# Weight and activation stores moved from SyncE's queue to GpSimd's, with a new instruction order

## The chip, the cores and the metric

The kernel runs on one core of a Trainium2 chip. The metric is the device time of one execution in microseconds (us); lower is better. The core has five engines with an instruction queue each: TensorE (PE, with its weight loads PEld), VectorE (DVE), ScalarE (ACT), GpSimd (POOL) and SyncE (SP). SyncE does nothing but issue transfers between the chip's memory (DRAM) and the on-chip buffers (SBUF); ScalarE and GpSimd can issue transfers too. Each queue runs strictly in its order: an instruction that waits holds back all behind it on its queue.

## The reference

Two layers, each with a windowed attention and a feed-forward part, on 2048 tokens of 1024 values, in bfloat16:

```python
x = x + A(layernorm(x)); x = x + B(layernorm(x))      # twice, with the same weights

def A(x):      # 32 heads of 32, window of 8 keys, 2 tokens apart
    q, k, v = split(x @ wqkv)
    logits[s, w] = (q[s] . k[s - 2 * w]) / sqrt(32)   # masked where s - 2 * w < 0
    o = sum over w of softmax(logits)[s, w] * v[s - 2 * w]
    return o @ wo

def B(x):
    return relu(x @ w1 + b1) ** 2 @ w2 + b2           # w1 is 1024 x 3584
```

## The kernel before

The tokens are split by parity, so that a window becomes eight neighbours, and worked on in blocks of 512: four blocks a layer, eight units `u` in all. A unit runs through layer norm and transposes (`SA`), the projections to q, k and v (`SQ`, `SQ7`), the attention on VectorE with logits and row sums on TensorE (`S2`), the output projection (`SW`, `SW7`), and the two feed-forward products (`SF1`, `SF2`). The attention of unit u + 1 is interleaved with the feed-forward part of unit u, so that VectorE and TensorE are both busy.

Most products use a form of Strassen's scheme with seven instead of eight sub-products. Its combined weights are made once, in units 0 and 1: VectorE forms four combinations of each weight tile in buffers named `tv` (`keep_wqkv`, `keep_w1`, `keep_w2`, `keep_wo`; at most four `tv` buffers live at a time), a store writes each to a scratch tensor in DRAM, and later units load them back from there into weight buffers `w`. The scratch tensors show in the profile as `sk` and `sqv` (q, k, v), `sw` (w1), `tw` (w2) and `two` (wo). The other stores are those of the layer's output: `xs` between the layers and `out_dram` at the end, both written from `xm` by `out_tile`, 128 tokens at a time; the last four token tiles are stored in halves of a row. There are 88 stores of scratch and 37 of layer outputs, some of these of half a row or less; the very last piece is issued from ScalarE, all others from SyncE.

In unit 0 the attention sums its products of q and k over the eight channel tiles with a tree of additions on VectorE before the logits' matmuls (`lg`) on TensorE. `DEP0` gives the depth of that tree for the first and the second half of the block: depth 2 leaves two sums, and so two times four matmuls, depth 3 one sum and four matmuls. All other units use depth 3 in both halves. The row sums of unit 0's softmax are matmuls as well (`den`).

No instruction is placed by hand. Every step is recorded in a `Plan` with its engine, a cost and what it reads and writes. `schedule` then plays the plan: at each moment a free engine takes the ready step of the lowest priority number for which buffers are free. A transfer may start only where at most `LANES` = 7 others have not landed by the plan's own reckoning, and it takes its bandwidth from one shared stream. `emit` first shifts priorities at random, by the seeds of `ORDER`, and replays; the seeds have been searched for a short plan. The order in which steps are taken is the order of each engine's queue in the program. So a changed cost or limit moves instructions on every engine. `dma` records a transfer; its argument `eng` names the issuing queue.

Of the kernel before, what the change touches and what calls it, by code (L numbers as in the profile page):

```python
# [45 lines left out]
KEEP = {"k": 0, "q": 1, "v": 1}  # L46
WO7 = (2, 3, 4, 5, 6)
KWO = 1
DEP0 = (2, 3)
NEARLY = 4  # L50
PLAIN1 = 1
HALF = 8
# [7 lines left out]
FNO = True  # L60
CPA = (1,)
AFTK = True
TAIL = True
CPT = ("xn3",)
PR1 = 20.0
# [3 lines left out]
GZ = 6  # L69

ORDER = [
# [9 lines left out]

MM = 0.2157
MMH = 0.1091
# [4 lines left out]
LANES = 7  # L88
# [45 lines left out]
class Plan:  # L134
# [45 lines left out]
    def schedule(self):  # L180
# [17 lines left out]
            fresh.add(item[2].eng)  # L198

        def fits(o):  # L200
            if o.mb and len(landed) >= LANES and landed[-LANES] > t + 1e-9:
                return False
            need = {}
            for b in o.bufs:
                if b.slot is None:
                    need[b.cls] = need.get(b.cls, 0) + 1
                    if b.tag in self.caps and (live.get(b.tag, 0) >= self.caps[b.tag] or b.idx != placed.get(b.tag, 0)):
                        return False
                    if b.bits == "seeded" and partial.issuperset(free["ps"]):
                        return False  # L210
            return all(len(free[c]) >= n for c, n in need.items())
# [15 lines left out]
            if o.ndep == 0:  # L227
                offer((o.prio, next(seq), o))
        dma_free = 0.0
        landed = []  # L230
        out = []
        t = 0.0
        left = len(self.ops)
        while left:
            progress = False
            for e in engs:
                if efree[e] > t + 1e-9 or e not in fresh:
                    continue
                i = next((i for i, item in enumerate(ready[e]) if fits(item[2])), None)
                if i is None:  # L240
                    fresh.discard(e)
                    continue
                o = ready[e].pop(i)[2]
                progress = True
                for b in o.bufs:
                    if b.slot is None:
                        take(b)
                efree[e] = t + o.dur
                end = t + o.dur
                if o.mb:  # L250
                    dma_free = max(dma_free, end) + o.mb / DMA_MBS
                    end = dma_free
                    landed.append(end + o.lat)
                out.append((t, len(out), o))
                left -= 1
                heapq.heappush(events, (efree[e], next(seq), None, False))
                if not o.mb:
                    heapq.heappush(events, (end + OWN_LAT.get(o.eng, 0.0), next(seq), o, True))
                heapq.heappush(events, (end + o.lat, next(seq), o, False))
# [5 lines left out]
            t, _, o, own = heapq.heappop(events)  # L265
# [72 lines left out]
class _Kernel:  # L338
# [84 lines left out]
    def dma(self, out, src, r, w, mb, prio=None, after=(), name="dma", cast=None, lat=None, eng="SP", dur=None):  # L423
        def fn():
            o = out()
            (self.nc.sync if eng == "SP" else self.nc.scalar).dma_start(o if cast is None else o.bitcast(cast), src())
        return self.p.add(eng, dur or 0.08, fn, r, w, self.nxt() if prio is None else prio, after, mb=mb, name=name, lat=lat)

    def par_tile(self, par_ap, t):
        cls = t // (self.NT // 2)  # L430
# [22 lines left out]
    def keep_w2(self, j0, n, w):  # L453
        nc, p = self.nc, self.p
        t = [Buf("2K", "tv", [128, 2, BLK], F16) for _ in range(4)]

        def raw(k2, n2):
            return w[:, k2, n2, :n]

        def comb(i, a, b, r):  # L460
            p.add("DVE", dve(n * BLK), lambda: nc.vector.tensor_tensor(t[i][:, :n], a(), b(), ALU.subtract), r, [(t[i], 0)], 45.0, name="tv")
            self.dma(lambda: self.tw[i][:, j0:j0 + n, :], lambda: t[i][:, :n], [(t[i], 0)], [(("tw", i), j0)], n * 0.13, prio=50.0, name="twst", lat=4.0)
        comb(0, lambda: raw(0, 1), lambda: raw(0, 0), [(w, 0)])
        comb(1, lambda: raw(1, 1), lambda: t[0][:, :n], [(w, 1), (t[0], 0)])
        comb(2, lambda: raw(1, 1), lambda: raw(0, 1), [(w, 0), (w, 1)])
        comb(3, lambda: raw(1, 0), lambda: t[1][:, :n], [(w, 1), (t[1], 0)])
# [56 lines left out]
    def keep_wqkv(self, nm, ws, after=()):  # L523
# [4 lines left out]
        def one(s):  # L528
# [5 lines left out]
            def comb(t, a, b, op, r, pr):  # L534
                p.add("DVE", dve(1024), lambda: nc.vector.tensor_tensor(t[:], a(), b(), op), r, [(t, 0)], self.nxt(), after, name="tq")
                i = COMB.index(pr)
                self.dma(lambda: self.scr[job][nm, s][:, i], lambda: t[:], [(t, 0)], [((job, nm, s), i)], 0.26, prio=50.0, name="wqst", lat=4.0)
            w0, w1 = (ws[0], s), (ws[1], s)
            comb(s1, lambda: raw(1, 0), lambda: raw(1, 1), ALU.add, [w1], 5)
            comb(s3, lambda: raw(0, 0), lambda: raw(1, 0), ALU.subtract, [w0, w1], 7)  # L540
# [130 lines left out]
    def keep_w1(self, dp, w):  # L671
# [5 lines left out]

        def store(pr, src, r):
            i = COMB.index(pr)
            self.dma(lambda: self.scr["w1"][dp][:, i], src, r, [(("w1", dp), i)], 0.26, prio=50.0, name="w1st", lat=4.0)  # L680
        s1, s3, s2, s4 = t = [Buf("2K", "tv", [128, 4, 256], F16) for _ in range(4)]

        def comb(t, a, b, op, r, pr):
# [419 lines left out]
    def keep_wo(self, wos):  # L1103
# [5 lines left out]
        for c0 in (0, 2):  # L1109
            t = [Buf("2K", "tv", [128, 2, BLK], F16) for _ in range(4)]  # L1110

            def comb(i, a, b, r, t=t, c0=c0):
                p.add("DVE", dve(1024), lambda: nc.vector.tensor_tensor(t[i][:], a(), b(), ALU.subtract), r, [(t[i], 0)], 45.0, name="tv")
                self.dma(lambda: self.two[i // 2][:, i % 2, c0:c0 + 2, :], lambda: t[i][:], [(t[i], 0)], [(("two", i // 2), (i % 2, c0))], 0.26,
                         prio=50.0, name="twst", lat=4.0)
            w0, w1 = (wos[0], 0), (wos[1], 0)
            comb(0, lambda c0=c0: raw(0, 1, c0), lambda c0=c0: raw(0, 0, c0), [w0])
            comb(1, lambda c0=c0: raw(1, 1, c0), lambda t=t: t[0][:], [w1, (t[0], 0)])
# [336 lines left out]
    def out_tile(self, layer, t, db, py, xm, end=False):  # L1455
# [19 lines left out]
            return  # L1475
        self.merge(py, lambda: xm[:, sl], lambda: o()[:, sl], [(xm, db)], [(xm, db)], "xo")
        if final and t >= self.NT - 4:
            self.dma(lambda: dst[:, sl], lambda: o()[:, sl], [(xm, db)], [(cell, db)], 0.14, prio=-10.0)
        elif t in self.half:
            self.dma(lambda: dst, lambda: o(), [(xm, 0), (xm, 1)], [(cell, 0), (cell, 1)], 0.27, prio=-10.0)  # L1480
            self.half.discard(t)
        else:
            self.half.add(t)
# [135 lines left out]
```

## Time and profile before

| | us |
|---|---|
| timed runs, median of 3 (lowest to highest) | 1136.02 (1134.17 to 1136.22) |
| the profiled execution's own time | 1131.52 |
| its span, first to last instruction | 1129.8 |
| TensorE busy (share of the span) | 1118.8 (99%) |
| VectorE busy | 990.3 (88%) |
| ScalarE busy | 824.1 (73%) |
| GpSimd busy | 1.8 (0%) |
| mean granted TensorE clock | 0.999 |
| moved by DMA, mean | 362.35 MB, 321 GB/s |

A page of the profile lists the busy time of each engine, groups of instructions by line, tiles and shapes (with the mean ns of one, the idle time of the engine before them, and what ended it), and transfers with the median time from issue to landing. Names such as `w<-tw` say what is written from what. `SPq` is SyncE's queue. The tables of waits name the waiting engine and line, the releaser, and then us in total, the number of waits and the longest. The busy time of matmuls overlaps the next one's, as their ends are modelled, so a mean of one is longer than its place in the row; a row of several in a timeline gives the place.

### The profile page before, as it was taken

How to read it: one execution, taken by the hardware profiler on the slowest of the kernel's cores; microseconds unless marked ns; L12 is line 12 of the kernel's file. 1: busy time of each engine (PE TensorE's matmuls, PEld its weight loads, DVE VectorE, ACT ScalarE, POOL GpSimd, SP SyncE). 2: the span in 40 equal slices, each digit the busy share in tenths (PEclk: the TensorE clock that was granted, in tenths of full speed). 3: DMA queues.
4: the chain of work that ended last, by engine and by line, in shares of the span. 5: the costliest groups of instructions: out<-in, count | busy, mean ns of one | idle time of the engine just before them, and what ended most of it. 6: DMA issues, size and time to landing. Idle time of an engine off the chain costs nothing.

```text
span 1129.8 us, 20632 instructions
## 1 busy us (share of the span) xinstructions
PE 1118.8 (99%) x7854; PEld 770.4 (68%) x7900; DVE 990.3 (88%) x1517; ACT 824.1 (73%) x1648; POOL 1.8 (0%) x8
## 2 busy tenths in 40 slices
PE   9999999999999999999999999999999999999998
PEld 6645764678746887468864788557884678845864
DVE  8999989999996999969999699997999899996341
ACT  7747995598975799567994769847798468933961
POOL 0000000000000000000000000000000000000000
PEclk9999999999999999999999999999999999999999
DMA  9956799999999986999789998999969999689981
GB/s 360 313 193 232 247 312 341 313 352 391 346 367 376 360 333 241 360 418 341 294 285 315 403 318 333 301 382 380 378 230 337 374 360 402 205 290 330 352 300 65
DMA packets 137022, 362.35 MB, mean 321 GB/s; under 512 B 67418, under 2 KB 68570, under 8 KB 116570
## 3 DMA queue, kind: packets, MB, share of 16 engines
q1 hardware_dynamic: 136778, 360.95, 91.4%
q8 instruction: 62, 1.02, 0.4%
q14 instruction: 38, 0.31, 0.1%
q10 hardware_dynamic: 144, 0.07, 0.0%
HBM read 314.84 MB, written 31.46 MB: 307 GB/s over the span
## 4 chain that ended last, share of the span: by engine, by line
PE 72%; DVE 15%; ACT 7%; DMA 3%; issue 2%; SPq 0%; DVEq 0%
PE X L667 19%; PE X L1393 12%; PE Z L667 10%; PE pq L893 6%; PE Z L1393 6%; PE Y L667 5%; PE py L1089 4%; DVE P L955 3%; PE Y L1393 3%; PE X L1160 3%; DVE P L963 3%; ACT r L1328 2%; DVE pr L1034 2%; PE Z L1160 1%; ACT rr L1334 1%
## 5 line engine op out<-in xcount | busy, mean ns | idle before, releaser
L667 PEld LDWEIGHTS <-w 128*128 128x128 f16 (+1 forms) x4904 | 479.8, 98 | 69.6 <-issue 0.5
L1393 PEld LDWEIGHTS <-r 128*128 128x128 f16 x1183 | 115.8, 98 | 135.4 <-issue 1.1
L1393 PE MATMUL X<-w,r 128*128 128x512 f16 (+2 forms) x782 | 176.3, 377 | 0.6 <-ACT X L502 0.2
L955 DVE TENSOR_TENSOR P<-q,k 128x2048 f16<-128x2048 f16 x128 | 154.4, 1230 | 2.4 <-ACT q L630 2.4
L667 PE MATMUL X<-T,w 128*128 128x256 f16 x1224 | 151.7, 273 | 0.0
L1034 DVE TENSOR_TENSOR pr<-pb,v 128x4096 f16<-128x4096 f16 x64 | 146.4, 2298 | 0.5 <-PE X L1393 0.2
L963 DVE TENSOR_TENSOR P<-P,P 128x2048 f16<-128x2048 f16 x111 | 136.1, 1228 | 0.2
L1328 ACT ACTIVATE r<-rr 128x1024 f16<-128x1024 f16 x110 | 123.8, 1137 | 0.3
L1041 DVE TENSOR_TENSOR pr<-pr 128x1024 f16<-128x1024 f16 (+1 forms) x128 | 118.0, 956 | 0.1
L667 PE MATMUL X<-TA,w 128*128 128x256 f16 x864 | 108.4, 273 | 0.0
L893 PE MATMUL pq<-xnA,w 128*128 128x256 f16 (+1 forms) x512 | 86.6, 326 | 1.3 <-DMA w<-in_A_wqkv_dram 0.8
L600 ACT COPY Y<-X 128x512 f32<-128x512 f32 x115 | 71.2, 619 | 18.8 <-PE X L667 14.9
L893 PEld LDWEIGHTS <-w 128*128 128x128 bf16 x512 | 49.7, 98 | 33.5 <-issue 1.3
L1307 ACT CAST y<-Z 128x512 f16<-128x512 f32 x110 | 68.8, 642 | 4.8 <-PE Z L667 4.8
L1311 DVE TENSOR_TENSOR rr<-u,y 128x512 f16<-128x512 f16 x110 | 46.3, 428 | 22.9 <-ACT y L1307 14.5
L1334 ACT ACTIVATE rr<-Y,b1T 128x256 f16<-128x256 f32 x110 | 55.4, 537 | 3.8 <-PE Y L667 3.2
L667 PE MATMUL Y<-xnB,w 128*128 128x256 f16 x440 | 56.4, 273 | 0.0
L1062 ACT CAST yxo<-X 128x512 f16<-128x512 f32 x27 | 15.4, 587 | 56.0 <-PE X L1393 56.0
L1334 ACT ACTIVATE rr<-X,b1T 128x256 f16<-128x256 f32 x110 | 55.2, 559 | 0.7 <-PE X L667 0.5
L618 ACT CAST u<-X 128x512 f16<-128x512 f32 x72 | 41.8, 587 | 18.8 <-PE X L667 17.4
L667 PE MATMUL X<-xnB,w 128*128 128x256 f16 x440 | 55.5, 273 | 0.0
L622 ACT CAST yq<-Z 128x512 f16<-128x512 f32 x72 | 41.9, 586 | 18.4 <-PE Z L667 18.0
(168 smaller groups left out, 1692.0 us busy)
## 6 DMA issues: line engine op xcount, KB each, us to landing
w<-sw SPq DMA_DIRECT2D x49, 1024.0 KB, 9.9
w<-tw SPq DMA_DIRECT2D x56, 896.0 KB, 6.8
w<-in_B_w_dram SPq DMA_DIRECT2D x42, 896.0 KB, 5.8
w<-in_B_w_dram SPq DMA_DIRECT2D x35, 1024.0 KB, 9.4
w<-in_A_wqkv_dram SPq DMA_DIRECT2D x32, 1024.0 KB, 9.9
w<-sqv SPq DMA_DIRECT2D x24, 1024.0 KB, 11.2
w<-in_B_w_dram SPq DMA_DIRECT2D x28, 512.0 KB, 6.5
w<-sk SPq DMA_DIRECT2D x12, 1024.0 KB, 7.8
```

Of the source, the lines that this page charges most:

```text
L600: self.p.add("ACT", act(512), lambda: self.nc.scalar.copy(Y[:], X[:]), [(X, 0)], [(Y, 0)], UP, name="u")
L667: nc.tensor.matmul(bank[:, a, :], lw[:, k, a * 128:(a + 1) * 128], rhs(k), start=(start and k == 0 and a == 0), stop=(k == 3), skip_group_ ...
L893: nc.tensor.matmul(pq[:, t0 * HB:t1 * HB], w[:, c0 // 2 % 2, kd // 4, kd % 4, c0 % 2 * 128:c0 % 2 * 128 + 128], xnT[:, 2 * t0:2 * t1, kd, ...
L955: nc.vector.tensor_tensor(cur[:], q[:, c, None, hb * HB:(hb + 1) * HB].to_broadcast([128, W, HB]), _win_ap(k[:, c, :], HALO + hb * HB, HB) ...
L963: nc.vector.tensor_tensor(other[:], other[:], cur[:], ALU.add)
L1034: p.add("DVE", dve(4096), lambda pr=pr, ch=ch: nc.vector.tensor_tensor(pr[:], pb[:].unsqueeze(1).to_broadcast([128, 2, W, HB]), _win_ap2(v ...
L1041: nc.vector.tensor_tensor(dst, pr[:, :, 0:n, :], pr[:, :, n:2 * n, :], ALU.add)
L1307: p.add("ACT", act(512), lambda: nc.scalar.copy(y[:], bank[:]), [(bank, 0)], [(y, 0)], 1.5, name="y")
L1311: p.add("DVE", dve(512), lambda: nc.vector.tensor_tensor(r[:, :, m, :], us[i][:], y[:], ALU.add), [(us[i], 0), (us[i], 1), (y, 0)], [(r, ( ...
L1328: p.add("ACT", 0.955, lambda: nc.scalar.activation(out=r2[:, f:f + 2, :].rearrange("p a t -> p (a t)"), in_=r[:].rearrange("p a m t -> p ( ...
L1334: p.add("ACT", 0.36, lambda a=a: nc.scalar.activation(out=r[:, a, 0, :], in_=bank[:, a, :], func=ACTF.Relu, bias=self.b1T[:, f + a:f + a + ...
L1393: nc.tensor.matmul(banks[q][:, lo:hi], left(jj, q), w[:, j, lo:hi], start=(start and jj == 0), stop=(jj == h - 1), skip_group_check=True)
```

## The change

The stores of the combined weights and of the layers' outputs are issued from GpSimd, except for those of the last two token tiles of the result. Loads and transposing transfers are then alone on SyncE's queue (with these last stores). In the plan, a transfer on GpSimd costs its queue 1.0 instead of 0.08 and lands later than before, and at most four of them are in flight; the limit of seven counts SyncE's and ScalarE's transfers alone. `DEP0` becomes (3, 3). The 111 seeds of `ORDER` are replaced by 122 others.

```diff
--- before.py
+++ after.py
@@ -46,7 +46,7 @@
 KEEP = {"k": 0, "q": 1, "v": 1}
 WO7 = (2, 3, 4, 5, 6)
 KWO = 1
-DEP0 = (2, 3)
+DEP0 = (3, 3)
 NEARLY = 4
 PLAIN1 = 1
 HALF = 8
@@ -60,6 +60,7 @@
 FNO = True
 CPA = (1,)
 AFTK = True
+ST = "POOL"
 TAIL = True
 CPT = ("xn3",)
 PR1 = 20.0
@@ -69,15 +70,16 @@
 GZ = 6
 
 ORDER = [
...
 
 MM = 0.2157
 MMH = 0.1091
@@ -198,7 +200,9 @@
             fresh.add(item[2].eng)
 
         def fits(o):
-            if o.mb and len(landed) >= LANES and landed[-LANES] > t + 1e-9:
+            mine = landed[o.eng == "POOL"]
+            n = 4 if o.eng == "POOL" else LANES
+            if o.mb and len(mine) >= n and mine[-n] > t + 1e-9:
                 return False
             need = {}
             for b in o.bufs:
@@ -227,7 +231,7 @@
             if o.ndep == 0:
                 offer((o.prio, next(seq), o))
         dma_free = 0.0
-        landed = []
+        landed = [], []
         out = []
         t = 0.0
         left = len(self.ops)
@@ -250,7 +254,7 @@
                 if o.mb:
                     dma_free = max(dma_free, end) + o.mb / DMA_MBS
                     end = dma_free
-                    landed.append(end + o.lat)
+                    landed[o.eng == "POOL"].append(end + o.lat)
                 out.append((t, len(out), o))
                 left -= 1
                 heapq.heappush(events, (efree[e], next(seq), None, False))
@@ -423,8 +427,8 @@
     def dma(self, out, src, r, w, mb, prio=None, after=(), name="dma", cast=None, lat=None, eng="SP", dur=None):
         def fn():
             o = out()
-            (self.nc.sync if eng == "SP" else self.nc.scalar).dma_start(o if cast is None else o.bitcast(cast), src())
-        return self.p.add(eng, dur or 0.08, fn, r, w, self.nxt() if prio is None else prio, after, mb=mb, name=name, lat=lat)
+            {"SP": self.nc.sync, "ACT": self.nc.scalar, "POOL": self.nc.gpsimd}[eng].dma_start(o if cast is None else o.bitcast(cast), src())
+        return self.p.add(eng, dur or (1.0 if eng == "POOL" else 0.08), fn, r, w, self.nxt() if prio is None else prio, after, mb=mb, name=name, lat=lat)
 
     def par_tile(self, par_ap, t):
         cls = t // (self.NT // 2)
@@ -459,7 +463,7 @@
 
         def comb(i, a, b, r):
             p.add("DVE", dve(n * BLK), lambda: nc.vector.tensor_tensor(t[i][:, :n], a(), b(), ALU.subtract), r, [(t[i], 0)], 45.0, name="tv")
-            self.dma(lambda: self.tw[i][:, j0:j0 + n, :], lambda: t[i][:, :n], [(t[i], 0)], [(("tw", i), j0)], n * 0.13, prio=50.0, name="twst", lat=4.0)
+            self.dma(lambda: self.tw[i][:, j0:j0 + n, :], lambda: t[i][:, :n], [(t[i], 0)], [(("tw", i), j0)], n * 0.13, prio=50.0, name="twst", lat=5.0 if ST == "POOL" else 4.0, eng=ST)
         comb(0, lambda: raw(0, 1), lambda: raw(0, 0), [(w, 0)])
         comb(1, lambda: raw(1, 1), lambda: t[0][:, :n], [(w, 1), (t[0], 0)])
         comb(2, lambda: raw(1, 1), lambda: raw(0, 1), [(w, 0), (w, 1)])
@@ -534,7 +538,7 @@
             def comb(t, a, b, op, r, pr):
                 p.add("DVE", dve(1024), lambda: nc.vector.tensor_tensor(t[:], a(), b(), op), r, [(t, 0)], self.nxt(), after, name="tq")
                 i = COMB.index(pr)
-                self.dma(lambda: self.scr[job][nm, s][:, i], lambda: t[:], [(t, 0)], [((job, nm, s), i)], 0.26, prio=50.0, name="wqst", lat=4.0)
+                self.dma(lambda: self.scr[job][nm, s][:, i], lambda: t[:], [(t, 0)], [((job, nm, s), i)], 0.26, prio=50.0, name="wqst", lat=5.0 if ST == "POOL" else 4.0, eng=ST)
             w0, w1 = (ws[0], s), (ws[1], s)
             comb(s1, lambda: raw(1, 0), lambda: raw(1, 1), ALU.add, [w1], 5)
             comb(s3, lambda: raw(0, 0), lambda: raw(1, 0), ALU.subtract, [w0, w1], 7)
@@ -677,7 +681,7 @@
 
         def store(pr, src, r):
             i = COMB.index(pr)
-            self.dma(lambda: self.scr["w1"][dp][:, i], src, r, [(("w1", dp), i)], 0.26, prio=50.0, name="w1st", lat=4.0)
+            self.dma(lambda: self.scr["w1"][dp][:, i], src, r, [(("w1", dp), i)], 0.26, prio=50.0, name="w1st", lat=5.0 if ST == "POOL" else 4.0, eng=ST)
         s1, s3, s2, s4 = t = [Buf("2K", "tv", [128, 4, 256], F16) for _ in range(4)]
 
         def comb(t, a, b, op, r, pr):
@@ -1112,7 +1116,7 @@
             def comb(i, a, b, r, t=t, c0=c0):
                 p.add("DVE", dve(1024), lambda: nc.vector.tensor_tensor(t[i][:], a(), b(), ALU.subtract), r, [(t[i], 0)], 45.0, name="tv")
                 self.dma(lambda: self.two[i // 2][:, i % 2, c0:c0 + 2, :], lambda: t[i][:], [(t[i], 0)], [(("two", i // 2), (i % 2, c0))], 0.26,
-                         prio=50.0, name="twst", lat=4.0)
+                         prio=50.0, name="twst", lat=5.0 if ST == "POOL" else 4.0, eng=ST)
             w0, w1 = (wos[0], 0), (wos[1], 0)
             comb(0, lambda c0=c0: raw(0, 1, c0), lambda c0=c0: raw(0, 0, c0), [w0])
             comb(1, lambda c0=c0: raw(1, 1, c0), lambda t=t: t[0][:], [w1, (t[0], 0)])
@@ -1475,9 +1479,9 @@
             return
         self.merge(py, lambda: xm[:, sl], lambda: o()[:, sl], [(xm, db)], [(xm, db)], "xo")
         if final and t >= self.NT - 4:
-            self.dma(lambda: dst[:, sl], lambda: o()[:, sl], [(xm, db)], [(cell, db)], 0.14, prio=-10.0)
+            self.dma(lambda: dst[:, sl], lambda: o()[:, sl], [(xm, db)], [(cell, db)], 0.14, prio=-10.0, eng=ST if t < self.NT - 2 else "SP")
         elif t in self.half:
-            self.dma(lambda: dst, lambda: o(), [(xm, 0), (xm, 1)], [(cell, 0), (cell, 1)], 0.27, prio=-10.0)
+            self.dma(lambda: dst, lambda: o(), [(xm, 0), (xm, 1)], [(cell, 0), (cell, 1)], 0.27, prio=-10.0, lat=3.5 if ST == "POOL" else None, eng=ST)
             self.half.discard(t)
         else:
             self.half.add(t)
```

In the program as built, 120 transfers move from SyncE's queue to GpSimd's: 28 `sw`, 28 `tw`, 16 `sqv`, 8 `sk`, 8 `two`, 16 `xs`, and 16 of `out_dram` (12 whole rows and 4 halves). TensorE has four `lg` matmuls fewer (64 for 68), VectorE one addition more in the tree (112 for 111). Each engine's other instructions are the same in kind and number, in another order.

19 rows, old and new, of the table ORDER are left out of this document.

## Prediction

> **What bounds the kernel now.** I read the busy parts of the page first, then the table by stages of 25 us, then who waited for whom on TensorE, and last the SyncE queue, on which the change works.
>
> ```profile
> span 1129.8 us, 20632 instructions
> PE 1118.8 (99%) x7854; PEld 770.4 (68%) x7900; DVE 990.3 (88%) x1517; ACT 824.1 (73%) x1648; POOL 1.8 (0%) x8
> ...
> 0.00:25.00 25.00, 22.34 (x176) 16.25 (x177) 19.84 (x36) 17.09 (x40) 1.76 (x8) 1.00 0.93 352
> 50.00:75.00 25.00, 24.89 (x124) 11.79 (x123) 25.00 (x28) 12.12 (x23) 0.00 (x0) 1.00 0.76 252
> 75.00:100.00 25.00, 24.89 (x121) 11.59 (x122) 25.00 (x32) 15.89 (x33) 0.00 (x0) 1.00 0.42 138
> 150.00:175.00 25.00, 24.89 (x143) 14.03 (x144) 21.95 (x34) 24.21 (x50) 0.00 (x0) 1.00 1.00 336
> 200.00:225.00 25.00, 23.48 (x160) 15.55 (x160) 24.91 (x38) 14.54 (x26) 0.00 (x0) 1.00 0.89 301
> 1125.00:1150.00 25.00, 1.14 (x11) 0.78 (x8) 0.85 (x2) 0.39 (x2) 0.00 (x0) 0.93 0.03 10
> ...
> PE py L1089 <- DMA w<-in_A_wo_dram: 1.4, 1, 1.4
> PE pk L1515 <- DVE ones L365: 1.1, 1, 1.1
> PE pq L893 <- DMA w<-in_A_wqkv_dram: 0.8, 1, 0.8
> PE pq L893 <- DVE xnA L816: 0.5, 1, 0.5
> ```
>
> In a stage row the pairs are PE, PEld, DVE, ACT and POOL busy, then the granted clock, the DMA share and GB/s. TensorE bounds nearly every stage: it idles 1129.8 - 1118.8 = 11.0 us in all. Of that 2.7 us lie in the first stage, 4.8 - 1.1 = 3.7 us behind the last matmul (the row counts from 1125 to the end at 1129.8), and 1.5 us between 200 and 225, where one wait of 1.4 us for the second half of `wo` makes nearly all of it. The other 43 stages share 3.1 us. So no reordering can win more than a few us, while a new wait costs its full length. VectorE is the second limit: full from 50 to 100 and again around 200. The edit acts almost only before 260 us, where the combined weights are formed and stored; behind that only the layer output's stores are left.
>
> **The SyncE queue**, from its waits, its issues, and the view of tile `tv` (ns minimum/median/maximum):
>
> ```profile
> SPq L426 <- PE X L667: 236.8, 94, 8.3
> SPq L426 <- DVE tv L535: 27.4, 11, 16.8
> SPq L426 <- DVE tv L684: 21.0, 16, 4.8
> SPq L426 <- DVE tv L461: 15.2, 14, 3.1
> ...
> w<-in_B_w_dram SPq DMA_DIRECT2D x42, 896.0 KB, 5.8
> w<-in_A_wo_dram SPq DMA_DIRECT2D x11, 1024.0 KB, 7.2
> sw<-tv SPq DMA_DIRECT2D x28, 256.0 KB, 4.9
> ...
> L426 SPq DMA_DIRECT2D sw<-tv x28: 319/326/1272, 99.2 to 154.0; - x28
> ```
>
> SyncE spends 236.8 us waiting for products to free weight buffers: that is loads sitting ready for room, which costs nothing. It also spends 27.4 + 21.0 + 15.2 = 63.6 us on stores that wait for VectorE to form `tv`, with loads queued behind them. This second part is what the change takes away.
>
> **The change part by part.** The sum is made against the profiled execution, 1131.52 us with a span of 1129.8; the median of the timed runs, 1136.02, is 4.5 us above it, and I add the difference to that median.
>
> *Stores to GpSimd.* 120 stores leave SyncE's queue (28 of them the row `sw<-tv` above, at 0.33 us of issue each) and stand on GpSimd's, which did eight instructions in the whole span. SyncE's saving, 120 x 0.33 = 39 us, is off the path: it waits for buffers far longer. In the built program each SyncE transfer waits for the one eight before it on the same queue; loads now have these eight places alone. A store that waits for `tv` or `xm` now holds back only stores. Who waits for those: VectorE, which needs one of four `tv` buffers back, and loads that read the scratch. The trace has no GpSimd store. From below, its issue is SyncE's 0.33 us; from above, the longest such issue, 1.27 us. Either fits: the densest stretch is the 28 `sw` stores in 154.0 - 99.2 = 54.8 us, one in 2.0 us. I take 0 us for the move itself, covered by these gaps; what it costs when they don't cover is the first rival.
>
> *Depth 3 for the first half of block 0* removes four `lg` matmuls and adds one tree addition. Both prices, and the surroundings of the logits now:
>
> ```profile
> L963 DVE TENSOR_TENSOR P<-P,P 128x2048 f16<-128x2048 f16 x111 | 136.1, 1228 | 0.2
> 98.29 1.73 PE py L1089 x8
> 224.38 1.75 PE X L667 x16
> ...
> 55.96 1.03 PE L970 MATMUL lg<-P,grp 128*128 128x512 f16 x4
> 57.10 3.61 PE L893 MATMUL pq<-xnA,w 128*128 128x512 f16 x16
> 60.55 1.04 PE L999 MATMUL den<-e,ident 128*128 128x256 bf16 x8
> ...
> 56.65 2.07 ACT L981 ACTIVATE e<-lg 128x512 bf16<-128x512 f32 x4
> ```
>
> A matmul of 512 columns takes a place of 1.73 / 8 = 0.216 us, one of 256 columns 1.75 / 16 = 0.109. Four fewer: -0.9 us. The addition is 1.23 us on a VectorE that is full from 50 to 100, but TensorE has the next block's projections to do there and idled 0.1 us per stage; between 0 and +1.2 I take +0.3.
>
> *The new order, block 0's second half.* Now 16 `pq` matmuls stand between the last `lg` and `den` (57.10 to 60.55), and the four exponentials that `den` reads end at 56.65 + 2.07 = 58.72, inside that cover. In the built order of the changed kernel the eight `den` matmuls follow the four `lg` at once. The last exponential is done 58.72 - 55.96 = 2.76 us after the first `lg` starts; the work until the last two `den` is 4 x 0.216 + 6 x 0.109 = 1.5 us. The cover is gone: +1.2 us (down to +0.8 if the exponentials start 0.4 us sooner than behind today's cast).
>
> *The new order, the end of block 1's key projection.* Two edits meet here.
>
> ```profile
> L618 ACT CAST u<-X 128x512 f16<-128x512 f32 x72 | 41.8, 587 | 18.8 <-PE X L667 17.4
> 211.68 9.04 DMA w<-in_A_wo_dram
> 220.76 1.02 PE L1089 MATMUL py<-w,o 128*128 128x512 bf16 x4 [1.42 <-DMA w<-in_A_wo_dram]
> ```
>
> First, the last two products into bank X now follow each other on TensorE, with ScalarE's copy `u` between them: 0.59 us and two hand-overs, +0.8 (from 0.6 to 1.0). Second, the load of the second half of `wo` is released by a product that is 40 matmuls of 256 columns and 4 of 512 ahead of its first use: 40 x 0.109 + 4 x 0.216 = 5.2 us, and 6.0 with the copy's wait. Such a load lands in 7.2 us (median), 9.0 at this place now, and the nearest shorter one, 896 KB, in 5.8. The new wait is then 0, 1.2 or 3.0 us; with half of the span between the two `wo` rows I take 2.0. Today's wait of 1.4 goes, since today's queue (store, store, load) is gone: -1.4. The next loads wanted there (`wqkv` and `sqv`) are released 8.7 us or more ahead and gain the same 2.8 us of waiting as cover, so nothing further is counted.
>
> *The start.* The second token tile's transposes are now in two parts with filler matmuls between, so its second copy comes about two fillers (0.4 us) later; VectorE, which does that copy, was late itself (the wait of 0.5 above): +0.2. The eight-place limit on SyncE binds nothing at the start. *The end.* The last two token tiles' stores stay on SyncE and ScalarE; the four half-row stores before them move to GpSimd, with the last product's 28 matmuls (6 us) over them: 0.
>
> Sum: -0.9 + 0.3 + 1.2 + 0.8 + 2.0 - 1.4 + 0.2 = **+2.2 us**: 1133.7 for a profiled execution, **1138.2** for the median. With the ends of the terms it reaches from 0 (`wo` lands in time) to +4.5.
>
> **Rivals.** *A store's round trip becomes VectorE's limit* (slower). Four `tv` buffers and one store per 2.0 us: from forming `tv` to the store's landing 8.1 us may pass. Now it is one combination and 4.9 us. For it:
>
> ```profile
> L684 DVE TENSOR_TENSOR tv<-w x14: 710/729/741, 98.3 to 149.8; 128x1024 f16<-128x1024 bf16 x14
> DVE tv L535 <- DMA sqv<-tv: 3.0, 1, 3.0
> L744 DVE TENSOR_SCALAR xn<-xm,sm 128x1024 f16<-128x1024 f16 x24 | 12.8, 538 | 1.2 <-ACT sm L741 1.2
> ```
>
> 0.73 + 4.9 = 5.6 us, so 2.5 us are spare, and VectorE did once wait 3.0 us for a store's landing. At 9.5 us the 28 stores take 28 x (9.5/4 - 2.03) = 10 us longer; less the 3 us that VectorE idles between 150 and 175, that is +7 on the forecast: **1145**. It decides above 8.1 us; four stores issued in a burst at 1.27 us each would add 3.8 us to the last one, which is enough. Against it: the loads' traffic no longer stands ahead of a store in its queue. The Trainium skill bears on it both ways. SBUF — State Buffer, section Who interferes with whom, says that VectorE's `tensor_scalar` and copies can lock GpSimd out of the port through which it writes a transfer's descriptors, and that `tensor_tensor` doesn't: by that, the 0.54 us of the row of L744 would be the most that one instruction adds to a store, and the many rows of `tensor_tensor` nothing. DMA: Bandwidth & Descriptors, Anatomy of one DMA, puts a GpSimd transfer at about 2.0 us and its bytes over 436 GB/s: by that a 256 KB store would be an estimated 2.6 us and this rival would not happen. No run here shows a GpSimd store yet.
>
> *The freed SyncE queue brings loads earlier* (faster). The 63.6 us of stores' waits ahead of loads are gone. The unprofiled runs hold 4.5 us that the profile doesn't show; if these are waits for loads and go, and `wo` lands in time, the sum is 0.2 - 4.5: **1131.7**; half of it gives 1134. For it: the largest single wait of TensorE in the steady state is for such a load. Against it: nothing shows those 4.5 us to be load waits, and in the built order more loads than before have under 10 us of matmuls between release and use (12 against 6), so what the queue gives is largely spent. The skill (same page, Issuing engines are not separate DMA queues) says that another issuing engine saves only the time to issue: by that this rival would be worth nothing, since the issue is off the path.
>
> That the stores would not move at all is excluded: the built program has 120 on GpSimd's queue.
>
> **How the numbers follow.** Forecast case (0 to +4.5 us) 0.50, round-trip rival 0.23, early-loads rival 0.27. A measurement of this kernel can tell about 0.2%, 2.3 us, from no change, so the line lies at 1138.3, through the forecast case: I give 0.28 of its 0.50 to "same" and 0.22 to "slower". Faster: 0.25 from the early loads (0.02 of that rival stays within 0.2%). Slower: 0.22 + 0.23 = 0.45. Same: 0.30. The forecast case's own range is 1136 to 1140.5; to leave out no more than 2 in 10 it is widened to 1132 (0.08 below) and 1144 (half of the round-trip rival, 0.12, above).
>
> **What would show it.** Right: TensorE's waits list about 1 us of `den` for `e`, 0.8 us of X for `u`, and 1 to 3 us of `py` for `wo` a little above 215; four fewer `lg`; no DVE wait for `tv` stores above 3 us. The round-trip rival shows as VectorE waiting for `sw<-tv` between 100 and 160 and TensorE's idle time rising there. The early-loads rival shows as no `wo` wait. I am wrong altogether if VectorE's instructions become longer beside GpSimd's stores, or if TensorE idles more behind 260 us, where hardly a store is left.

## The result and the profile after

| | before | after |
|---|---|---|
| median of 4 runs | 1135.24 us | 1142.94 us |
| range | 1134.17 to 1136.22 | 1142.26 to 1145.99 |
| profiled execution / its span | 1131.52 / 1129.8 | 1143.27 / 1141.6 |

The change makes the kernel slower by 0.8%: ratio 1.008, 95% interval 1.0058 to 1.0101 (the quotient of the two medians, 1.0068, lies in it). The forecast was +2.2 us, and it became +7.7, inside the range but three and a half times the forecast.

First the page of the changed kernel and its table by stages, with the columns as before the change; then rows of the kernel before (TensorE alone): the last two are of the same stages, the others serve further below.

```profile
span 1141.6 us, 20738 instructions
PE 1123.5 (98%) x7896; PEld 769.8 (67%) x7896; DVE 990.2 (87%) x1518; ACT 822.3 (72%) x1648; POOL 66.8 (6%) x128
...
50.00:75.00 25.00, 21.07 (x104) 9.94 (x102) 25.00 (x27) 13.24 (x28) 1.62 (x3) 1.00 0.76 232
...
225.00:250.00 25.00, 21.72 (x146) 13.87 (x144) 11.76 (x21) 18.67 (x40) 4.37 (x9) 1.00 1.02 352
250.00:275.00 25.00, 22.63 (x196) 18.92 (x195) 21.95 (x34) 19.10 (x40) 3.06 (x6) 1.00 1.06 327
```

```profile
25.00:50.00 25.00, 25.00 (x183) 1.00 1.09 324
...
100.00:125.00 25.00, 25.00 (x204) 1.00 0.86 293
125.00:150.00 25.00, 25.00 (x204) 1.00 0.81 264
...
225.00:250.00 25.00, 24.90 (x183) 1.00 1.07 360
250.00:275.00 25.00, 25.00 (x228) 1.00 1.06 369
```

TensorE has holes in two places: 3.9 us between 50 and 75 (0.1 before) and 3.3 + 2.4 us between 225 and 275 (0.1 before). Behind 350 us it is as full as before. Who waited for whom, and how the transfers landed (median us from issue to landing in the last column of the second view), say what is late:

```profile
PE py L1093 <- DMA w<-in_A_wo_dram: 2.4, 1, 2.4
PE Z L671 <- DVE T L707: 2.4, 1, 2.4
PE den L1003 <- DVE e L995: 1.7, 1, 1.7
PE lg L974 <- DVE P L967: 1.5, 1, 1.5
...
PE X L671 <- ACT u L622: 0.7, 1, 0.7
...
PE den L1003 <- ACT e L985: 0.6, 1, 0.6
...
DVE T L707 <- DMA xnB<-xn: 4.9, 3, 2.9
...
DVE tv L465 <- DMA tw<-tv: 1.8, 1, 1.8
```

```profile
w<-in_A_wqkv_dram SPq DMA_DIRECT2D x32, 1024.0 KB, 10.8
w<-in_A_wo_dram SPq DMA_DIRECT2D x11, 1024.0 KB, 8.4
sw<-tv POOLq DMA_DIRECT2D x28, 256.0 KB, 4.1
tw<-tv POOLq DMA_DIRECT2D x28, 256.0 KB, 7.1
...
L430 POOL DMA_DIRECT2D sw<-tv x28: 539/539/542, 103.8 to 164.9; - x28
L688 DVE TENSOR_TENSOR tv<-w x14: 682/687/690, 102.8 to 160.1; 128x1024 f16<-128x1024 bf16 x14
```

The forecast's own waits are there: `wo`, `u`, `den` for the exponentials. Beside them VectorE is late for `e`, `P` and `T`. VectorE's instructions have not become longer (687 ns here, 729 before), and a store holds GpSimd for 0.54 us, so neither of these is the reason. The loads on SyncE take longer: `wo` 8.4 us against 7.2, though most of that belongs to the new order, in which they take 8.2 from the old queue too (run e1 below). The earliest trace of the queue itself is ScalarE at the start, waiting for the second token tile (timeline, idle time in brackets; the kernel before, where it waits for the first, then e1, whose order is that of the changed kernel, then the changed one):

```profile
17.97 1.06 ACT L750 ACTIVATE xn<-xt 128x1024 f16<-128x1024 bf16 x1 [0.35 <-DMA xt<-in_A_x_dram]
```

```profile
19.29 1.06 ACT L754 ACTIVATE xn<-xt 128x1024 f16<-128x1024 bf16 x1
```

```profile
22.57 1.06 ACT L754 ACTIVATE xn<-xt 128x1024 f16<-128x1024 bf16 x1 [4.05 <-DMA xt<-in_A_x_dram]
```

### The profile page after: what moved, and what is told of

It is laid out like the page before. It is cut to its first block, busy times and chain, and to the rows that moved or that the text cites. A ratio compares the mean times of both kernels' runs of the same rounds, so it can differ in the third digit from the quotient of the medians.

```text
span 1141.6 us, 20738 instructions
## 1 busy us (share of the span) xinstructions
PE 1123.5 (98%) x7896; PEld 769.8 (67%) x7896; DVE 990.2 (87%) x1518; ACT 822.3 (72%) x1648; POOL 66.8 (6%) x128
## 3 DMA queue, kind: packets, MB, share of 16 engines
q8 instruction: 62, 1.02, 0.4%
## 4 chain that ended last, share of the span: by engine, by line
PE 79%; ACT 4%; DVE 4%; DMA 2%; issue 1%; DVEq 0%; ACTq 0%
PE X L671 24%; PE X L1397 14%; PE Z L671 12%; PE Z L1397 7%; PE Y L671 6%; PE py L493 4%; PE Y L1397 3%; PE X L1164 3%; PE py L1093 2%; PE Z L1164 2%; DMA xnB<-xn 1%; DMA w<-sqv 1%; DVE P L959 1%; ACT rr L1338 1%; ACT r L1332 1%
## 5 line engine op out<-in xcount | busy, mean ns | idle before, releaser
L1066 ACT CAST yxo<-X 128x512 f16<-128x512 f32 x27 | 15.6, 585 | 52.5 <-PE X L1397 52.5
## 6 DMA issues: line engine op xcount, KB each, us to landing
w<-sw SPq DMA_DIRECT2D x49, 1024.0 KB, 10.8
w<-in_A_wqkv_dram SPq DMA_DIRECT2D x32, 1024.0 KB, 10.8
```

## The experiments

Ratios are to the kernel before, timed beside each run on the same chip; its median there was 1132.97 us for e1 to e4, 1134.51 for e5 to e8, 1134.23 for e9 to e12 and 1132.95 for e13 to e15. In each, "GpSimd" and "SyncE" say from which queue a store is issued; the plan and every engine's order otherwise stay those of the kernel named.

**Order or queue.** The first theory put the loss into the new order. Two kernels part it from the queue: the new order with its stores issued from SyncE, and the old order with all 120 stores issued from GpSimd.

```diff
 after:  -"POOL": self.nc.gpsimd}[eng].dma_start
         +"POOL": self.nc.sync}[eng].dma_start
 before: +def dma(..., to=None):   ...[to or eng].dma_start(...)
         +to="POOL" in every store but those of the last two token tiles
```

> The changed kernel's order on every engine, but each store is issued from SyncE at its place in that order. If the loss lies in the new order (theory), TensorE keeps its waits for the logits' sum and for den near 53 to 61 us, and the time stays near 1143 or rises by the few us that loads then stand behind stores. If the loss comes from issuing on GpSimd (rival), it falls back to about 1135.

> The kernel before with its own plan and order; only the 120 stores are issued from GpSimd, the queue of each engine is otherwise the same. Theory (loss in the order): 1133.5 to 1136, the wait of 1.4 us for wo near 220 us gone or shorter, since the load no longer stands behind stores that wait for VectorE. Rival (loss in the queue): about 1143, with VectorE waiting for stores.

Measured: order alone 1136.67 us, ratio 1.003 (1.0018 to 1.0043); queue alone 1142.03, ratio 1.0077 (1.0059 to 1.0096). The queue alone, which the prediction had at 0 us, costs as much as the whole change. The order, searched for this queue, costs 0.3% without it.

**Is VectorE's lateness the cause?** Two spots where VectorE was late were relieved in the changed kernel: its loads of the two biases were put on GpSimd's queue, so that `b2b` lands sooner, and the third tree addition was left out.

```diff
 e3: -[eng].dma_start   +["POOL" if name == "b" else eng].dma_start
 e4: +if u == 0 and hb == 0 and lvl == 2:
     +    def fa():
     +        pass
```

> The changed kernel, but the two small loads of b1 and b2 are issued from GpSimd, free at that time, instead of behind eleven loads on SyncE. VectorE waits 1.75 us for b2 at 21.5 us in the changed kernel. Theory (VectorE is late by what it lost before 50 us): this wait goes, and TensorE's waits between 50 and 62 us fall from 3.7 to about 2, the time to about 1141.3. Rival (TensorE's waits there have their own cause in the order of den behind lg): 1143.

> The changed kernel without the added addition of block 0's first half (left out: the sum of the first four channel tiles in these logits); order and everything else as changed. Theory (VectorE sets TensorE's waits between 50 and 62 us, and the addition is wholly on its path): 1.1 to 1.2 us faster, about 1141.8. Rival (the addition is covered by the projections): 1143.

Measured: 1142.56, ratio 1.0077 (1.0061 to 1.0094), and 1142.51, ratio 1.008 (1.0063 to 1.0097). Neither moves the time by more than the intervals can tell. With the bias early, TensorE's wait for `e` fell from 1.7 to 0.5 us, and the same product that starts at 353.39 us in the changed kernel's profile starts at 352.44, 0.95 us earlier (0.45 without the addition). So the theory fell as the main cause: what these two spots add to VectorE's lateness is at most about 1 us of the 11.8 by which the profiled execution is longer.

**Do the freed loads run too far ahead?** Without stores in between, SyncE issues loads sooner. A placeholder of one row (2 KB) took each store's old place on SyncE, with the same waits.

```diff
+if to == "POOL":                     # e8: eng == "POOL", in the changed kernel
+    one = src()[0:1]
     ...
+    rest = self.tc.dram_tile(list(one.shape), one.dtype, name=f"ph{self.nph}")
+    self.nc.sync.dma_start(rest[:], one)
```

> The kernel before, its plan and order, stores issued from GpSimd as in e2_old_order_new_queue, and beside that SyncE issues, at each store's old place, a transfer of one row (2 KB) of the same tile, so that loads again stand behind the wait for VectorE and share the eight places with it. If the loss comes from loads that run ahead and fill the transfer engines (theory): most of it goes, 1133 to 1136 with the kernel before at 1133. If it comes from GpSimd's transfers themselves (rival): it stays at 1142, and the transposes of unit 1 land in 14 us as in e2 (9.8 in the kernel before).

> The changed kernel, stores on GpSimd, with the one-row transfers on SyncE at each store's place in its order. Theory (loads that run ahead): it falls to the time of the new order on the old queue, ratio to the kernel before 1.003 to 1.004. Rival (GpSimd's transfers themselves): ratio stays at 1.008.

Measured: 1144.64, ratio 1.0087 (1.006 to 1.0115), and 1144.67, ratio 1.0083 (1.0057 to 1.0108). With SyncE's places kept the loss stays. At the start this is clean: ScalarE's wait for `xt` is 3.2 us in e5, 2.9 in e2, so the loads' earlier issue isn't what makes it. Further on the placeholders cost something themselves (TensorE's wait for `wo` is 6.7 us in e5, 3.0 in e2; VectorE waits 3.4 us for a placeholder in e8), and a gain of a few us could hide behind that.

**Which stores?** In the old order, four subsets on GpSimd: all but the 24 qkv stores; these 24 alone; these without the first four; and the 60 of w1 products and rows alone.

```diff
 e6:  to="POOL" on w1st, twst, two, xs and out
 e7:  to="POOL" on wqst
 e11: as e7, the first four calls on SyncE   (+[to if to and self.nst > 4 else eng])
 e12: to="POOL" on w1st, xs and out
```

> As e2_old_order_new_queue, but the 24 stores of the combined q, k, v weights are issued from SyncE as before; the other 96 from GpSimd. In e2, 7.4 of 9.9 us are lost before 70 us, where these are the only stores. Theory (the loss is made where freed loads compete at the start): 1135 to 1137, the 7 us back. Rival (each store on GpSimd costs its share): 24 of 120 stores, so 7 of the 9 us stay, 1140.

> The reverse: the kernel before with only these 24 stores issued from GpSimd. Theory: 1139 to 1140 (the loss of the start, less what later stages absorb). Rival (share by number of stores): 1135.

> The kernel before, with the qkv weights' stores 5 to 24 on GpSimd and the first four, of 11 to 19 us, left on SyncE. If the loss of the 24 starts where ScalarE waits 2.2 us for xt at 18 us, pushed back by those four stores: that wait falls to under 0.6, the first ph comes 2 us or more earlier than with all 24 (113.4 us; before 109.9), and the time is 1136 to 1138. If every store adds its share: 20 of 24 remain, 1139 to 1140.5. If the first four have nothing to do with it: 1140.5.

> The kernel before, with only the w1 products' stores (103 to 165 us), the rows between the layers and the output rows moved to GpSimd; the qkv, w2 and wo products' stores stay on SyncE. Theory 'a store costs where the loads behind it are late already': no TensorE wait for a DMA stands in that stretch, so 1134 to 1136, equal to before within 0.2%. Rival 'by number': 96 stores without the qkv ones cost 3.6 us, these some 50 would cost 1.9, 1136 to 1137. If the new queue frees SyncE for loads that matter: below 1133.

| GpSimd issues | us | ratio |
|---|---|---|
| 96 stores, not qkv (e6) | 1138.13 | 1.0034 (1.0018 to 1.0049) |
| 24 qkv stores (e7) | 1140.57 | 1.0049 (1.0032 to 1.0066) |
| 20 of them (e11) | 1136.2 | 1.0019 (1.0009 to 1.003) |
| 60 stores, w1 and rows (e12) | 1133.23 | 0.9993 (0.9983 to 1.0004) |

The loss doesn't go by number: 60 stores cost nothing, 24 cost half a per cent, and 20 of these 0.19%. That the first four make the larger part is likely by the medians, but not beyond the intervals. As the 60 are free, e6's 0.34% should belong to its 36 stores of w2 and `wo` products, if such costs add up; TensorE's wait for `wo` was 4.4 us there, 1.4 before. The stretch in which the four are issued, 12 to 24 us, shows why (transfers issued in it; the kernel before, then e7):

```profile
DMA packets 1698, 4.85 MB, mean 404 GB/s; under 512 B 200, under 2 KB 200, under 8 KB 1697
...
w<-in_A_wqkv_dram SPq DMA_DIRECT2D x4, 1024.0 KB, 9.8
sk<-tv SPq DMA_DIRECT2D x4, 256.0 KB, 8.9
```

```profile
DMA packets 1529, 4.87 MB, mean 406 GB/s; under 512 B 216, under 2 KB 216, under 8 KB 1528
...
w<-in_A_wqkv_dram SPq DMA_DIRECT2D x3, 1024.0 KB, 15.4
sk<-tv POOLq DMA_DIRECT2D x4, 256.0 KB, 7.9
```

Both move 4.9 MB at 405 GB/s. What differs is who gets it: from GpSimd the stores land in 7.9 us, and the loads that SyncE queued take 15.4. A part of the 15.4 is that SyncE, free of the stores, issues these loads earlier; counted from the start of the execution they land 0.9 to 1.8 us later than before. That a store overtakes a load which was queued first stands in e7's trace (timeline of both issues, the landing of this store, and what the two queues moved from 18 to 20 us: packets, MB, share; q0 is GpSimd's queue, q1 SyncE's):

```profile
8.91 1.61 SPq L426 DMA_DIRECT2D xt<-in_A_x_dram  x2
12.49 0.70 POOL L426 DMA_DIRECT2D sk<-tv  x1 [9.65 <-DVE tv L535]
...
sk<-tv POOLq DMA_DIRECT2D x1, 256.0 KB, 6.6
...
q0 software_dynamic: 117, 0.41, 51.6%
q1 hardware_dynamic: 150, 0.39, 48.6%
```

The store issued at 12.49 us is there at 19.1; the `xt` issued at 8.91 is there at 20.4, after 11.5 us. Before, and in e11, it took 9.6. In e11 ScalarE's wait for `xt` at the start was 0.33 us (2.21 in e7), as expected, and the time fell into the expected bracket. The `ph` named there didn't come earlier, though: 113.6 us (113.4 in e7). The next tile, whose load was issued at 23.4 us, just behind the first store left on GpSimd (23.0), was then the late one; that this store made it late isn't shown:

```profile
37.10 1.06 ACT L752 ACTIVATE xn<-xt 128x1024 f16<-128x1024 bf16 x1 [2.63 <-DMA xt<-in_A_x_dram]
```

**GpSimd's kind of queue, or any other queue?** The 24 qkv stores went to ScalarE's queue instead, and a kernel of its own measured the transfers by themselves.

```diff
 e10: to="ACT" on wqst
 e9:  per stretch: barrier; SyncE: 4 loads of 1 MB, x (256 KB), 2 loads of 1 MB;
      4 stores of 256 KB: none | on SyncE behind x | on GpSimd | on ScalarE; or 3 transposes on SyncE with the same
```

> The kernel before, with only the 24 stores of the qkv weights moved, to ScalarE's queue (a hardware queue as SyncE's is) where the earlier run moved them to GpSimd's (+0.49%). Theory 'a queue of its own goes beside': the same as GpSimd's, 1138 to 1141 us; the 1 MB qkv loads land in 12 to 14 us (before 9.9 over all, 9.5 in the crowded start) and ScalarE waits over 1.5 us for xt at the start (before 0.35). Rival 'the software queue slows the engines': 1133 to 1136, loads in 10, xt wait under 0.6. ScalarE itself pays 24 issues of some 0.33 us, 8 us of its time, which lies in the loss if it shows as waits of TensorE for ScalarE.

> A kernel of its own that leaves out the whole computation: in each of four rounds it starts, after a barrier, eight stretches. In the first four, SyncE issues four loads of 1 MB, a load x of 256 KB and two more loads of 1 MB, and four stores of 256 KB are left out (none), queued on SyncE behind x (sync), or issued at the start from GpSimd (pool) or from ScalarE (act). In the other four, SyncE issues three transposes of 256 KB with the same four stores. Theory 'a queue of its own goes beside': whatever engine issues them, stores on another queue move at once and overtake the loads that stand queued on SyncE's. Then x lands in pool and in act later than in none by up to 1.05 MB / 410 GB/s = 2.5 us, in sync as in none; pool and act are alike (within 0.7 us), and the last load lands alike in sync, pool and act. Rival 'the software queue slows the engines': x lands in act as in sync, or late by under half of what pool shows, the stretch with pool is the longest, and the transposes are slower beside pool alone.

From ScalarE: 1140.27 us, ratio 1.0065 (1.0049 to 1.0082), no better than from GpSimd. Its profile isn't clean: the qkv loads landed in 9.9 us over all, not in the 12 to 14 expected, and TensorE also waits 2.1 us for ScalarE's `py`. ScalarE's wait for `xt` is over the expected 1.5 us (2.7), but by luck: SyncE issued this load 2.6 us later than before, ahead of any such store, and it landed 9.4 us after its issue, no later than before (9.6). So e10 shows that the move to ScalarE's hardware queue isn't cheaper in time, not by which path. The transfers by themselves show more (second of four rounds; timeline of VectorE, which touches each load once it has landed; issue from SyncE, GpSimd, ScalarE):

```profile
178.42 2.03 SPq L28 DMA_DIRECT2D wsync<-in_B_w_dram  x4
191.91 0.16 DVE L43 COPY small<-xsync 128x1 bf16<-128x1 bf16 x1 [0.57 <-DMA xsync<-in_A_x_dram]
199.61 0.16 DVE L43 COPY small<-wsync 128x1 bf16<-128x1 bf16 x1 [2.49 <-DMA wsync<-in_B_w_dram]
199.94 1.97 SPq L28 DMA_DIRECT2D wpool<-in_B_w_dram  x4
216.07 0.16 DVE L43 COPY small<-xpool 128x1 bf16<-128x1 bf16 x1 [0.49 <-DMA xpool<-in_A_x_dram]
221.03 0.16 DVE L43 COPY small<-wpool 128x1 bf16<-128x1 bf16 x1 [2.32 <-DMA wpool<-in_B_w_dram]
221.40 2.25 ACTq L31 DMA_DIRECT2D back<-st  x4
237.04 0.16 DVE L43 COPY small<-xact 128x1 bf16<-128x1 bf16 x1 [0.48 <-DMA xact<-in_A_x_dram]
242.00 0.16 DVE L43 COPY small<-wact 128x1 bf16<-128x1 bf16 x1 [2.31 <-DMA wact<-in_B_w_dram]
```

From the start of its stretch, `x` is there after 13.5 us with the stores behind it on SyncE (13.6 without stores), after 16.1 beside GpSimd's and 15.6 beside ScalarE's: 2.6 and 2.1 us later (2.5 to 2.8 and 1.5 to 2.7 in the four rounds). The whole stretch takes 21.2, 21.1 and 20.6 us. So nothing is slower as a sum; a store on another queue doesn't line up behind SyncE's loads, it takes part of the transfer engines at once. It makes little difference whose queue it is. Here GpSimd's and ScalarE's stores are issued ahead of `x`, so these stretches show the sharing; that a load queued first is overtaken is shown by e7 above.

The Trainium skill has this rule: DMA: Bandwidth & Descriptors, Queues, rings and completion order, says that each transfer engine takes turns between the queues that have work, a packet at a time. The runs agree: 2.6 and 2.1 us for 1.05 MB that otherwise came behind. The same page's Issuing engines are not separate DMA queues, which the prediction cites against its early-loads rival, says that transfers of all issuing engines interleave, and that another issuing engine saves only the time to issue. The first half agrees with e9. Taken by the second alone, e7 would be without effect, and it costs 0.49%. The measurement decides: the order in which transfers land changes too.

**The rule turned round.** If a queue of its own overtakes, a late load can be put there. In e12, six loads of `wo` of 1 MB, among them the one whose wait stands in every kernel, were issued from GpSimd too.

```diff
-  ...self.wo[:, 2048 * g:2048 * (g + 1)]..., [(w, 0)], 1.06, name="w")
+  ...self.wo[:, 2048 * g:2048 * (g + 1)]..., [(w, 0)], 1.06, name="w", to="POOL")
```

> The kernel before with the w1 stores and the rows on GpSimd (1133.2), and the loads of wo, too, issued from GpSimd: now these loads overtake what stands queued on SyncE (at 200 to 206 us four tw stores hold it for 5.7 us). If the place behind waiting stores makes the load late, TensorE's wait for it (2.0 us, 1.4 in the kernel before) falls under 0.5 and the time to 1131 to 1132.5. If its buffer comes free that late anyway, the wait and the time stay (1133 to 1134). If the loads that it overtakes are then late themselves: over 1134.

Measured: 1140.64 us, ratio 1.0065 (1.0048 to 1.0081), the third of the outcomes named. Two lines of issue (GpSimd, then SyncE) and two of waiting:

```profile
33.42 0.87 POOL L426 DMA_DIRECT2D w<-in_A_wo_dram  x1 [30.58 <-DMA xt<-in_A_x_dram]
...
34.41 1.14 SPq L426 DMA_DIRECT2D w<-in_A_wqkv_dram  x2
...
51.35 0.69 DVE L535 TENSOR_TENSOR tv<-w 128x1024 f16<-128x1024 bf16 x1 [5.65 <-DMA w<-in_A_wqkv_dram]
...
56.91 1.86 PE L999 MATMUL den<-e,ident 128*128 128x256 bf16 x8 [4.50 <-DVE e L991]
```

Two `wo` loads, wanted much later and issued at 45 us before, now go out beside two `wqkv` loads and share the engines with them; VectorE stands 5.65 us for these, all that is queued on it stands too, and TensorE loses 4.5 us at `den`. The wait for `wo`, now near 228 us, stayed at 2.2 us: the load that it waits for left GpSimd at 219.02, 0.34 us after the store ahead of it, when a product freed its buffer. So there the place in the queue wasn't what held it.

**Back to the changed kernel.** In its own order the qkv stores, then all but those of w1 and the rows, went back to SyncE.

```diff
 e13: +["SP" if name in ('wqst',) else eng].dma_start
 e14: +["SP" if name in ('wqst', 'twst') else eng].dma_start
```

> The changed kernel with its 24 qkv stores issued from SyncE, at their places in its own order. If what it lost beyond its order (1142.9 against 1136.7) comes from stores that overtake the loads queued on SyncE, most in the crowded first 70 us: ScalarE's wait for xt at 22.6 us goes from 4.05 to under 1, and the time to 1138 to 1140. If the crowded start is not where this order loses: 1142 to 1143.

> The changed kernel with its qkv, w2 and wo products' stores on SyncE; only the w1 products' stores and the rows are on GpSimd. By the same theory these 60 cost nothing, and what is left is the new order alone: 1135.5 to 1138, as the run with the new order on the old queue (1136.7). If a store costs by number: 1139 to 1140.

Measured: 1142.2, ratio 1.0077 (1.0063 to 1.0092), and 1139.28, ratio 1.0055 (1.0041 to 1.007). The first expectation failed: ScalarE's wait for `xt` is gone from the profile and the last `den` comes at 59.2 instead of 61.9 us, but the time gains nothing that the interval can tell. So the crowded start isn't where this order loses in the timed runs. The second lies between the order alone (1.003) and the whole change (1.008), above the 1135.5 to 1138 of the theory: a part comes back with the w2 and `wo` stores, and what remains above the order alone is at the edge of the two intervals. In microseconds it lies in the bracket of "a store costs by number". On the old order e12 excludes that reading; on this order no run does.

## Why the prediction was wrong

- **The step that failed** is the term "0 us for the move itself", with the reason that issue time lies in gaps and that a store on GpSimd holds back only stores. The first half held (0.54 us per store, inside the bracket of 0.33 to 1.27 us). The second didn't: a store that stands behind loads on SyncE also lands behind them, and on its own queue it doesn't. The prediction saw one side of this ("the loads' traffic no longer stands ahead of a store in its queue", for the round-trip rival) and put nothing for the other, that the stores then take time from these loads. On the old order the term is 1142.03 - 1132.97 = 9.1 us; on the new one it is the difference between ratios 1.008 and 1.003, 0.5% or some 5.7 us. This mechanism was none of the rivals.
- **The sum of the other terms**, +2.2 us, belongs to the new order: measured alone, +0.3%, 3.7 us, with an interval of 2.0 to 4.9. The sum lies in it. Single terms: `den` for the exponentials 0.6 (1.2 forecast), X for `u` 0.7 (0.8), `wo` 2.4 in place of 1.4 (2.0), and exactly 2.0 in the order alone. The tree addition at +0.3: leaving it out moved the time by less than can be told.
- **The round-trip rival** fell: the `sw` stores, for which its limit of 8.1 us was worked out, land in 4.1 us, earlier than before (4.9); the `tw` ones land in 7.1, with their combination 7.8, and VectorE waits once, 1.8 us, for one (3.4 in the order alone).
- **The early-loads rival** has the opposite sign: qkv loads land in 10.8 us over all, 10.2 in the order alone and 9.9 before, and keeping SyncE's places doesn't win the time back. That the freed queue was worth nothing was right, for the wrong reason. The 4.5 us between the profiled execution and the median, on which this rival drew, likely go in part with TensorE's clock: of the executions of the kernel before beside e1 to e4, the eleven with a mean granted clock of 1.000 took 1132.4 us on average, the four with 0.998 took 1136.2.
- **One reading was too high**: of TensorE's 11.0 us of idle time before, some 4 to 5 are, by estimate, no idle time. The profile lacks 46 matmuls (7854 for 7900 weight loads; e15, with all 7900, has 3.6 us more busy time), and each leaves a hole of 0.11 us. No term of the sum is taken from it.
- **What would have shown it beforehand**: the stage rows of the start with a DMA share of 0.93 (0 to 25 us) and 1.09 (25 to 50). Where the transfer engines are full, a transfer that moves forward moves another one back, as in e7.

Open: in the changed kernel's own order the loss beyond the order isn't assigned to single stores. The qkv stores explain 2.7 us up to 60 us in the profiled executions, but not in the timed ones (e13), and the holes between 225 and 275 us come and go with every variant. That the queue makes `xt` late there too is shown, as it is on time with the same order in e1 and e13. That it makes the holes behind 225 us is only likely: `xnB` is later (VectorE waits 4.9 us for it, 3.2 in e1), but `wo` is nearly as late in the order alone (TensorE waits 2.0 us for it there, 2.4 here). A second path, by the transposes of the last section, wasn't parted from it.

## What to carry to other kernels

A queue is also an order. Before a transfer is moved to another engine's queue, look for the stretch in which it is issued and for who waits for the loads queued there. With the DMA share near 1 it takes its part from these loads, and whoever already waits for one of them pays, as at the start and, by e6's trace, at `wo`. It cost nothing with room, as most of the w1 stores had (0.86 and 0.81 between 100 and 150 us), and also for 24 of the 32 rows, which e12 issues at a share of 1.02 to 1.07: a full share alone doesn't decide. Here only the move of those and of the rows was free (0.9993, 0.9983 to 1.0004), and no version beat the kernel before.

## What the hardware showed unexpectedly

In the kernel of transfers alone, SyncE's transposes take longer to issue beside another queue's stores (ns minimum/median/maximum of the issue):

```profile
L58 SPq DMA_TRANSPOSE tnone<-turn x12: 1258/1317/1347, 124.9 to 480.0; - x12
L58 SPq DMA_TRANSPOSE tpool<-turn x12: 1252/2131/3832, 140.8 to 497.0; - x12
L58 SPq DMA_TRANSPOSE tact<-turn x12: 1283/2332/2492, 150.5 to 507.0; - x12
```

Issuing one holds SyncE for 1.3 us alone and 2.1 to 2.3 us beside GpSimd's or ScalarE's stores, with the next loads behind it; it lands after 3.3, 5.6 and 4.9 us. In the kernels the second transpose, near 35 us, holds SyncE for 6.2 us before and for 5.5 and 6.4 in e6 and e12, which issue nothing on the other queue until then, but for 7.7, 10.0 and 10.7 in e7, e2 and e15 (5.9 in e11). So a queue beside SyncE's may make its loads late by this path too.

The turns between the queues go by packet rather than by byte (the transfers alone, from 228 to 230 us; packets, MB, share; q1 is SyncE's queue, q10 ScalarE's):

```profile
q1 hardware_dynamic: 101, 0.70, 82.5%
q10 hardware_dynamic: 100, 0.17, 22.5%
```

Both move 100 packets, SyncE's loads 4 times the bytes, as their rows of 8 KB and the stores' rows of 2 KB would have it.

And a hole in TensorE's work can cost more than its length. In e2 (TensorE's busy time, then the granted clock, the DMA share and GB/s):

```profile
225.00:230.00 5.00, 1.98 (x13) 1.00 1.02 414
230.00:235.00 5.00, 5.00 (x22) 0.66 1.01 423
```

Behind 3.0 us of idle time the granted clock is 0.66 for 5 us, which is another 1.7 us by estimate. It doesn't follow every hole: in the changed kernel's profile the clock stays at 1.00 there.
